# Splitting the last four down-projections of batch 0, with the up-projection's runs side by side

## The chip, the cores and the metric

The kernel runs on one core of a Trainium2 chip. Five engines work there side by side, each with its own queue in order: TensorE (PE) multiplies matrices, VectorE (DVE) and ScalarE (ACT) work elementwise, GpSimd (POOL) does so too but more slowly, and SyncE (SP) issues the transfers (DMA) from memory. The metric is the device time of one execution in microseconds (us). The kernel before takes 740.15 us, the median of three runs (739.81 to 740.30).

## The reference

An attention through a small pack, followed by a feed-forward layer with the Mish activation, all in float32:

```python
def sm_attn(qq, kk, vv):                       # softmax attention
    s = scale * np.matmul(qq, kk.transpose(0, 1, 3, 2))
    a = np.exp(s - np.max(s, axis=-1, keepdims=True))
    a = a / (np.sum(a, axis=-1, keepdims=True) + 1e-09)
    return np.matmul(a, vv)
p_packed = sm_attn(p, k, v)                    # p: 8 x 8 x 32 x 64
attn = sm_attn(q, p_packed, p_packed)          # q, k, v: 8 x 8 x 576 x 64
x = attn.transpose(0, 2, 1, 3).reshape(4608, 512)
h = x @ w_in                                   # w_in: 512 x 2048
g = h * np.tanh(np.log1p(np.exp(h)))           # Mish (h itself in the softplus above 20)
out = g @ w_out                                # w_out: 2048 x 512
```

The two weights arrive as float64 and are narrowed to float32 by the kernel.

## The kernel before

**Blocks.** The hidden width of 2048 is cut into 16 groups f of 128 columns (`NF`). One block t is the work for one group of one batch: t = 16 b + f. A block computes the up-projection of its group (`Group.up`, two runs: columns 0 to 255 and 256 to 575 of the batch's 576 tokens, into the two PSUM tiles `ps_h`), the Mish on ACT (`mish`, into `act`; the last 64 tokens go to `g_rest`), and the down-projection of an earlier group (`down(dn, c)`, four products c = 0 to 3 of 128 tokens each, accumulated in `acc` over all 16 groups). The earlier group lies one block back up to t = 16 and two blocks back from then on (`lag`).

**Two forms of a product.** Where `hi` and `lo` exist, an operand is split into a rounded part and the remainder, and three products in the type float32r (hi·hi, hi·lo, lo·hi; lines 801 to 803, and 763 for the up-projection) stand for one float32 product. Batch 0 has its down-projection in plain float32 (line 821, two instructions for each product); from batch 1 on it is split: `halves` makes `hi` and `lo` of `act` on DVE, and `split_wo(i)` makes those of group i's output weights, hi on ACT (line 114) and lo on DVE (line 115), at t = 16 + i.

**Packed weights.** The second attention has only 32 packed values for each head, so that x @ w_in is a product of its weights `aT_hi`, `aT_lo` with packed weights `wp` (packed values times w_in). `packed_half` makes them for batch 0 in every odd block (line 681 on PE, then `wp_hi` on ACT and `wp_lo` on DVE, lines 713 and 714), `packed_w` for four groups at a time for the later batches (lines 692 and 693). The PSUM pool `ps_a` has two tiles, which the packing and the attention share.

**Weights of batch 0.** The 32 pieces of w_in and w_out come in while batch 0 runs. Each passes a staging tile `w_st` of a ring of `STB` = 8 (SP, lines 641 and 675), is unpacked by `words` (ACT, lines 650 and 651; POOL, 652 and 656) and put together by `join` (DVE, lines 662 and 667). `join(n)` ends with `fetch(n + STB)`: a piece's tile is free when its `words` are done. At block t stand `join(2t + 5)` and, at the block's end, `words(2t + 9)`; pieces are counted from 0 here.

**Attention of batch 1.** It is a generator, advanced at marked places of the blocks t = 4 to 14 (three times in an even block, once in an odd one). Its loads of q, k and v stand in the same SP queue as the weights: k in t = 0 and 2, q and v in t = 4 and 5. Among its steps: the first exponentials at the end of t = 6, the second ones (`rise`, line 303) in t = 13, and in t = 14 the sum, the division, and for each of two head groups the transpose back (line 335), `upper` (ACT, line 338, `aT_hi`) and `lower` (DVE, line 341, `aT_lo`).

**Order.** PE's order is the program's throughout. Up to t = 15 that of the other engines is so too (`by_hand`); from then on a planner orders them. A block of t = 4 to 15 is written as: down 0, up run 0, advance, join, down 1, packed weights (odd blocks), down 2, advance, up run 1, halves, words, down 3, and an advance at the end of even blocks.

Of the kernel before, what the change touches and what calls it, by code (L numbers as in the profile page):

```python
# [17 lines left out]
GB = 3  # L18
KVB = 8
KQB = 5  # L20
STB = 8
WB = 4
# [7 lines left out]
HALFWAY = 8  # L30
SPLIT0 = 14
TOGETHER = 2
# [8 lines left out]
def body(  # L41
# [55 lines left out]
    PARTS = (slice(0, QC), slice(QC, S))  # L97
    wi = [[const.tile([P, 2, 2, QC], F32, name=f"wi{c}_{g}") for g in range(2)] for c in range(DF // FC)]
    stage = ExitStack()
    stg = stage.enter_context(tc.tile_pool(name="stg", bufs=STB, side="right"))  # L100
    late = []
# [6 lines left out]
    def split_wo(i):  # L108
        if i < HALFWAY:
            wo_hi[i], wo_lo[i] = [late[0].tile([P, DO], F32R, name=f"wo_{x}{i}") for x in ("hi", "lo")]  # L110
        else:
            wo_hi[i], wo_lo[i] = wo_slot(F32R, "wo_hi"), wo_slot(F32R, "wo_lo")
        both = [
            nc.scalar.copy(out=wo_hi[i], in_=wo[i]),
            nc.vector.tensor_tensor(out=wo_lo[i], in0=wo[i], in1=wo_hi[i].bitcast(F32), op=ALU.subtract),
        ]
        for x in both:
            tc.keep_in_program_order(x)

# [254 lines left out]
    class Later(Batch):  # L374
# [254 lines left out]
        def rest_rows(self):  # L629
            return out[self.b * S + MAIN:(self.b + 1) * S, :]  # L630

    class Weight:

# [5 lines left out]
        def fetch(self):  # L639
            self.st = stg.tile([P, 2 * FC], I32, name="w_st")  # L640
            nc.sync.dma_start(
                out=self.st.rearrange("p (m x) -> p m x", m=2),
                in_=w_in_v[:, 2 * self.g:2 * self.g + 2, self.n * FC:(self.n + 1) * FC],
            )
            self.dst = wi[self.n // 2][self.g][:, self.n % 2].rearrange("p m x -> p (m x)")
# [23 lines left out]
    class WeightOut(Weight):  # L669
# [3 lines left out]
        def fetch(self):  # L673
            self.st = stg.tile([P, 2 * FC], I32, name="w_st")
            nc.sync.dma_start(out=self.st, in_=w_out_v[:, self.i, :])
            self.dst = wo[self.i] = wo_slot(F32, "wo32")
# [49 lines left out]

    def split_tiles(name="g", bufs=GB):
        return [late[0].tile([P, MAIN], F32R, name=f"{name}_{n}", bufs=bufs) for n in ("hi", "lo")]

    def split(*srcs):  # L730

        hi, lo = split_tiles("r", 1)
        for n, src in enumerate(srcs):
            h, l = (x.rearrange("p (f u t) -> p u f t", u=len(srcs), f=src.shape[1])[:, n] for x in (hi, lo))
            nc.scalar.copy(out=h, in_=src)
            nc.vector.tensor_tensor(out=l, in0=src, in1=h.bitcast(F32), op=ALU.subtract)
        return hi, lo

    class Group:
# [50 lines left out]

        def halves(self):
            if self.b == 0:
                return
            self.g = split_tiles()
            hi, lo = self.g
            nc.vector.tensor_copy(out=hi, in_=self.act)  # L796
            nc.vector.tensor_tensor(out=lo, in0=self.act, in1=hi.bitcast(F32), op=ALU.subtract)  # L797
# [17 lines left out]
    def down(grp, c):  # L815
        b, f = grp.b, grp.f
        if f == 0 and c == 0:
            accs[:] = [ps_acc.tile([P, DO], F32, name=f"acc{i}", tag="acc") for i in range(NCH)]
        cs = slice(c * P, (c + 1) * P)
        if b == 0:  # L820
            nc.tensor.matmul(out=accs[c], lhsT=grp.act[:, cs], rhs=wo[f], start=f == 0, stop=f == NF - 1)  # L821
        else:
            down_one(accs[c], grp.g[0], grp.g[1], cs, f, f == 0, f == NF - 1)
        if f < NF - 1:
            return
        o = evac(accs[c], c)
        for dst, lo, hi in batches[b].rows(c):
            nc.sync.dma_start(out=dst, in_=o[lo:hi, :])
# [85 lines left out]
    with tc.manual_schedule(engines={mybir.EngineType.PE}):  # L914
# [53 lines left out]
        for t in range(n_groups + LAG):  # L968
# [28 lines left out]
            if t == NF:  # L997
                by_hand.close()
            if t == SPLIT0:
                stage.close()  # L1000
                late.append(ctx.enter_context(tc.tile_pool(name="late", bufs=1, side="right", reuse_waits="tile")))
            if 0 <= t - NF < NF:
                split_wo(t - NF)
            chunk = b == 0 and f % 2 == 1 and f < NF - 1
            if t == 0:
# [12 lines left out]
                join(3)  # L1018
            if dn:
                down(dn, 0)  # L1020
            if 2 <= t < FLOATS:
                grp.up_floats((0,), (0, 1))
                first.upper(t - 2)
            elif grp and t >= FLOATS:
                grp.up(0)
# [4 lines left out]
            if t <= 13:  # L1030
                join(2 * t + 5 + t // 12)
            if dn:
                down(dn, 1)
            if chunk:
                if t < FLOATS - 1:
                    packed_floats(f // 2 + 1, 0)
                    wps[0, f // 2 + 1] = packed_floats(f // 2 + 1, 1)
                else:
                    wps[0, f // 2 + 1] = packed_half(f // 2 + 1)
            if dn:  # L1040
                down(dn, 2)
            if t:
                advance(gen)
            if 2 <= t < FLOATS:
                grp.up_floats((1,), (0, 1))
                first.lower(t - 2)
            elif grp and t >= FLOATS:
                grp.up(1)
# [7 lines left out]
            if last:  # L1056
                flush()
                down_rest(dn)
            if dn:
                down(dn, 3)  # L1060
# [40 lines left out]
```

## Time and profile before

| | |
|---|---|
| median of three runs | 740.15 us |
| profiled execution: time | 739.97 us |
| its span, from the first instruction to the last | 738.2 us |
| granted TensorE clock over the span | 0.999 |
| DVE busy, of the span | 57% |
| ACT busy, of the span | 40% |
| POOL busy | 54.7 us, all before 111 us |
| float32 products of batch 0 (line 821) | 128 instructions, 63.7 us busy |

The page of a profile gives the busy time of each engine first. PE's busy time includes time in which a product waits in the pipeline, so its share alone does not tell whether PE is the limit; its waits and the chain of work that ended last tell that. The chain is followed back from the last instruction, at each step to what released it, or to the instruction before it on the same engine; its pieces are counted from the end of one to the end of the next. The span lies inside the execution's time; 1.77 us are outside it.

Batch 0 covers the first 130 us. The 16 DMA engines are at least 94% busy in each window of 20 us up to 100 us and at most 51% in the windows of 20 us from there to 200 us.

### The profile page before, as it was taken

How to read it: one execution, taken by the hardware profiler on the slowest of the kernel's cores; microseconds unless marked ns; L12 is line 12 of the kernel's file. 1: busy time of each engine (PE TensorE's matmuls, PEld its weight loads, DVE VectorE, ACT ScalarE, POOL GpSimd, SP SyncE). 2: the span in 40 equal slices, each digit the busy share in tenths (PEclk: the TensorE clock that was granted, in tenths of full speed). 3: DMA queues.
4: the chain of work that ended last, by engine and by line, in shares of the span. 5: the costliest groups of instructions: out<-in, count | busy, mean ns of one | idle time of the engine just before them, and what ended most of it. 6: DMA issues, size and time to landing. Idle time of an engine off the chain costs nothing.

```text
span 738.2 us, 12575 instructions
## 1 busy us (share of the span) xinstructions
PE 725.0 (98%) x5140; PEld 558.6 (76%) x5140; DVE 424.4 (57%) x727; ACT 296.5 (40%) x692; POOL 54.7 (7%) x71
## 2 busy tenths in 40 slices
PE   8899999999999999999999999999999999999997
PEld 7555555778887878887887878878788787888885
DVE  4998778848646465455734566373834638342332
ACT  4866745544433343252522425343422425232221
POOL 0585440000000000000000000000000000000000
PEclk9999999999999999999999999999999999999999
DMA  9999960735004540144202451043101100010002
GB/s 244 307 275 242 297 112 16 149 55 111 1 16 94 87 79 1 58 72 98 33 1 72 72 110 21 36 87 65 33 1 44 29 2 1 0 58 1 1 1 71
DMA packets 186601, 56.32 MB, mean 76 GB/s; under 512 B 173488, under 2 KB 175792, under 8 KB 186544
## 3 DMA queue, kind: packets, MB, share of 16 engines
q1 hardware_dynamic: 186544, 55.53, 31.9%
q8 instruction: 40, 0.66, 0.4%
q14 instruction: 17, 0.14, 0.1%
HBM read 46.07 MB, written 9.44 MB: 75 GB/s over the span
## 4 chain that ended last, share of the span: by engine, by line
PE 94%; DVE 2%; ACT 2%; DMA 1%; issue 1%; SPq 0%; ACTq 0%; DVEq 0%
PE ps_h L763 26%; PE acc L801 15%; PE acc L803 14%; PE acc L802 14%; PE acc L821 6%; PE ps_w L681 4%; PE ps_s L444 2%; PE ps_rest L803 2%; PE ps_rest L802 2%; PE ps_rest L801 2%; PE ps_h L510 1%; PE ps_h L885 1%; PE ps_h L775 1%; DMA w_st<-in_moe_w_in_dram 1%; PE ps_a L491 1%
## 5 line engine op out<-in xcount | busy, mean ns | idle before, releaser
L785 ACT ACTIVATE g<-ps_h 128x256 f32<-128x256 f32 (+2 forms) x256 | 97.5, 384 | 302.5 <-PE ps_h L763 282.4
L801 PE MATMUL acc<-wo_hi,g_hi 128*128 128x512 f32 x448 | 181.3, 405 | 0.0
L803 PE MATMUL acc<-wo_hi,g_lo 128*128 128x512 f32 x448 | 177.1, 395 | 0.0
L802 PE MATMUL acc<-wo_lo,g_hi 128*128 128x512 f32 x448 | 176.8, 395 | 0.0
L763 PE MATMUL ps_h<-aT_hi,wp_hi 128*128 128x256 f32 x496 | 157.3, 317 | 0.4 <-ACT g L785 0.4
L796 DVE CAST g_hi<-g 128x512 fp32r<-128x512 f32 x112 | 47.5, 424 | 184.7 <-ACT g L785 184.4
L763 PE MATMUL ps_h<-aT_lo,wp_hi 128*128 128x256 f32 x496 | 146.3, 295 | 0.0
L763 PE MATMUL ps_h<-aT_hi,wp_lo 128*128 128x256 f32 x496 | 146.2, 295 | 0.0
L801 PEld LDWEIGHTS acc<-wo_hi,g_hi 128*128 128x128 f32 x448 | 84.2, 188 | 40.3 <-issue 20.8
L763 PEld LDWEIGHTS ps_h<-aT_hi,wp_hi 128*128 128x128 f32 x496 | 93.4, 188 | 18.0 <-issue 6.1
L763 PEld LDWEIGHTS ps_h<-aT_lo,wp_hi 128*128 128x128 f32 x496 | 93.5, 188 | 14.5 <-issue 5.7
L803 PEld LDWEIGHTS acc<-wo_hi,g_lo 128*128 128x128 f32 x448 | 84.1, 188 | 21.5 <-DVE g_lo L797 2.0
L763 PEld LDWEIGHTS ps_h<-aT_hi,wp_lo 128*128 128x128 f32 x496 | 93.5, 188 | 0.0
L802 PEld LDWEIGHTS acc<-wo_lo,g_hi 128*128 128x128 f32 x448 | 84.1, 188 | 9.2
L797 DVE TENSOR_TENSOR g_lo<-g,g_hi 128x512 fp32r<-128x512 f32 x112 | 77.3, 690 | 5.8
L821 PE MATMUL acc<-wo,g 128*128 128x512 f32 x128 | 63.7, 605 | 1.0 <-DVE wo L667 0.6
L693 DVE TENSOR_TENSOR wp_lo<-ps_w,wp_hi 128x512 fp32r<-128x512 f32 x56 | 36.1, 684 | 17.6 <-ACT wp_hi L692 17.6
L692 ACT CAST wp_hi<-ps_w 128x512 fp32r<-128x512 f32 x56 | 30.1, 591 | 36.9 <-PE ps_w L681 36.9
L681 PE MATMUL ps_w<-wi,ppT 64*32 64x512 f32 (+1 forms) x576 | 37.9, 553 | 2.4 <-DVE wi L667 2.4
L821 PEld LDWEIGHTS acc<-wo,g 128*128 128x128 f32 x128 | 21.5, 189 | 18.8 <-issue 12.7
L787 ACT ACTIVATE g_rest<-ps_h 128x64 f32<-128x64 f32 x128 | 28.2, 220 | 0.0
L803 PE MATMUL ps_rest<-wo_hi,r_lo 128*128 128x512 f32 x64 | 25.2, 393 | 0.0
(125 smaller groups left out, 726.7 us busy)
## 6 DMA issues: line engine op xcount, KB each, us to landing
w_st<-in_moe_w_in_dram SPq DMA_DIRECT2D x16, 512.0 KB, 7.8
w_st<-in_moe_w_out_dram SPq DMA_DIRECT2D x16, 512.0 KB, 6.9
k_n<-in_k_dram SPq DMA_DIRECT2D x56, 144.0 KB, 3.2
q_n<-in_q_dram SPq DMA_DIRECT2D x56, 144.0 KB, 3.1
v_n<-in_v_dram SPq DMA_DIRECT2D x56, 128.0 KB, 2.9
out_dram<-o SPq DMA_DIRECT2D x28, 256.0 KB, 2.0
k_t<-in_k_dram SPq DMA_DIRECT2D x4, 288.0 KB, 4.6
v_t<-in_v_dram SPq DMA_DIRECT2D x4, 288.0 KB, 7.5
```

The lines of the kernel that those rows point to most:

```text
L681: nc.tensor.matmul(out=ps[h * NP:(h + 1) * NP, :], lhsT=ppTb[row:row + D, g, h * NP:(h + 1) * NP], rhs=w[row:row + D], start=True, stop=Tr ...
L692: nc.scalar.copy(out=hi, in_=ps)
L693: nc.vector.tensor_tensor(out=lo, in0=ps, in1=hi.bitcast(F32), op=ALU.subtract)
L763: nc.tensor.matmul(out=ps, lhsT=w[:, fs], rhs=a[:, g, cs], start=(n == 0), stop=(n == 5))
L785: nc.scalar.activation(out=self.act[:, a:a + m], in_=ps[:, :m], func=AF.Mish)
L787: nc.scalar.activation(out=self.g_rest[self.b % 2][self.f // 4][:, self.f % 4, :], in_=ps[:, m:n], func=AF.Mish)
L796: nc.vector.tensor_copy(out=hi, in_=self.act)
L797: nc.vector.tensor_tensor(out=lo, in0=self.act, in1=hi.bitcast(F32), op=ALU.subtract)
L801: nc.tensor.matmul(out=acc, lhsT=hi[:, cs], rhs=wh, start=start, stop=False)
L802: nc.tensor.matmul(out=acc, lhsT=hi[:, cs], rhs=wl, start=False, stop=False)
L803: nc.tensor.matmul(out=acc, lhsT=lo[:, cs], rhs=wh, start=False, stop=stop)
L821: nc.tensor.matmul(out=accs[c], lhsT=grp.act[:, cs], rhs=wo[f], start=f == 0, stop=f == NF - 1)
```

## The change

- **Down-projection.** The groups f = 12 to 15 of batch 0 (`PAIRS0` = 12) use the split form. Their output weights are split at t = 12 to 15, hi on ACT and lo on POOL, into tiles of the pool `kept`; `halves` makes hi of `act` on ACT and lo on DVE in these blocks. The splits at t = 28 to 31 go away.
- **Order.** In t = 4 to 16 both up runs stand behind down 1. In t = 13 to 16 the down-projection is in two parts: down 0 and 1 behind the join and the weights' split, down 2 and 3 at the block's end.
- **Staging.** The ring has 7 tiles in place of 8, four of them in the pool `kept` and three in `gpairs`; the first are used again for the split output weights of f = 12 to 15, the second for `hi` and `lo` of `act` in all later blocks.
- **Join.** At t = 9 one piece less is joined at the usual place, and that piece behind the packed weights.
- Split output weights of groups 0 to 3, in place of 0 to 7, have tiles of their own; the others use the tiles that float32 weights leave.

```diff
-STB = 8
+STB = 7
+KEPT = 4
...
-SPLIT0 = 14
+PAIRS0 = 12
+LATE0 = 14
...
+    kept = ctx.enter_context(tc.tile_pool(name="kept", bufs=KEPT, side="right"))
+    gpairs = ctx.enter_context(tc.tile_pool(name="gpairs", bufs=STB - KEPT, side="right"))
     stage = ExitStack()
-    stg = stage.enter_context(tc.tile_pool(name="stg", bufs=STB, side="right"))
+    stg = stage.enter_context(tc.tile_pool(name="stg", bufs=WB, side="right"))
...
     def split_wo(i):
-        if i < HALFWAY:
+        if i >= PAIRS0:
+            both = kept.tile([P, 2, DO], F32R, name="wo_pair", tag="w_st")
+            wo_hi[i], wo_lo[i] = both[:, 0], both[:, 1]
+        elif i < HALFWAY - KEPT:
             wo_hi[i], wo_lo[i] = [late[0].tile([P, DO], F32R, name=f"wo_{x}{i}") for x in ("hi", "lo")]
         else:
             wo_hi[i], wo_lo[i] = wo_slot(F32R, "wo_hi"), wo_slot(F32R, "wo_lo")
         both = [
             nc.scalar.copy(out=wo_hi[i], in_=wo[i]),
-            nc.vector.tensor_tensor(out=wo_lo[i], in0=wo[i], in1=wo_hi[i].bitcast(F32), op=ALU.subtract),
+            (nc.gpsimd if i >= PAIRS0 else nc.vector).tensor_tensor(
+                out=wo_lo[i], in0=wo[i], in1=wo_hi[i].bitcast(F32), op=ALU.subtract
+            ),
         ]
...
+    fetched = []
+
+    def staged():
+        fetched.append(1)
+        pool = kept if (len(fetched) - 1) % STB < KEPT else gpairs
+        return pool.tile([P, 2 * FC], I32, name="w_st", tag="w_st")
...
-    def split_tiles(name="g", bufs=GB):
-        return [late[0].tile([P, MAIN], F32R, name=f"{name}_{n}", bufs=bufs) for n in ("hi", "lo")]
+    def split_tiles(pool, name, tag=None):
+        both = pool.tile([P, 2, MAIN], F32R, name=name, tag=tag or name)
+        return both[:, 0], both[:, 1]
...
         def halves(self):
+            if self.b == 0 and self.f < PAIRS0:
+                return
+            self.g = split_tiles(gpairs, "g_pair", "w_st")
+            hi, lo = self.g
             if self.b == 0:
-                return
-            self.g = split_tiles()
-            hi, lo = self.g
-            nc.vector.tensor_copy(out=hi, in_=self.act)
+                nc.scalar.copy(out=hi, in_=self.act)
+            else:
+                nc.vector.tensor_copy(out=hi, in_=self.act)
             nc.vector.tensor_tensor(out=lo, in0=self.act, in1=hi.bitcast(F32), op=ALU.subtract)
...
-        if b == 0:
-            nc.tensor.matmul(out=accs[c], lhsT=grp.act[:, cs], rhs=wo[f], start=f == 0, stop=f == NF - 1)
+        if b == 0 and f < PAIRS0:
+            nc.tensor.matmul(out=accs[c], lhsT=grp.act[:, cs], rhs=wo[f], start=f == 0, stop=False)
...
-            if 0 <= t - NF < NF:
+            if 0 <= t - NF < PAIRS0:
                 split_wo(t - NF)
...
-            if dn:
+            late_down = dn and dn.b == 0 and dn.f >= PAIRS0
+            if dn and not late_down:
                 down(dn, 0)
...
-            elif grp and t >= FLOATS:
+            elif grp and t > NF:
                 grp.up(0)
             if chunk:
                 flush()
             else:
                 advance(gen)
             if t <= 13:
-                join(2 * t + 5 + t // 12)
+                join(2 * t + 5 + t // 12 - (t == 9))
+            if PAIRS0 <= t < NF:
+                split_wo(t)
+            if late_down:
+                down(dn, 0)
             if dn:
                 down(dn, 1)
+            if grp and FLOATS <= t <= NF:
+                grp.up(0)
+                grp.up(1)
             if chunk:
...
                     wps[0, f // 2 + 1] = packed_half(f // 2 + 1)
-            if dn:
+                    if t == 9:
+                        join(2 * t + 5)
+            if dn and not late_down:
                 down(dn, 2)
             if t:
                 advance(gen)
...
-            elif grp and t >= FLOATS:
+            elif grp and t > NF:
                 grp.up(1)
             if grp:
                 grp.halves()
...
+            if late_down:
+                down(dn, 2)
             if dn:
                 down(dn, 3)
```

More of the change, by code (lines that the diff above doesn't have):

```diff
@@ L114, in split_wo @@
             nc.scalar.copy(out=wo_hi[i], in_=wo[i]),
-            nc.vector.tensor_tensor(out=wo_lo[i], in0=wo[i], in1=wo_hi[i].bitcast(F32), op=ALU.subtract),
-        ]
-        for x in both:
-            tc.keep_in_program_order(x)
+            (nc.gpsimd if i >= PAIRS0 else nc.vector).tensor_tensor(
+                out=wo_lo[i], in0=wo[i], in1=wo_hi[i].bitcast(F32), op=ALU.subtract
+            ),
+        ]
+        if i < PAIRS0:
+            for x in both:
+                tc.keep_in_program_order(x)
     w_in_v = w_in.bitcast(I32).rearrange("(m p) f -> p m f", p=P)
@@ L639, in fetch @@
         def fetch(self):
-            self.st = stg.tile([P, 2 * FC], I32, name="w_st")
+            self.st = staged()
             nc.sync.dma_start(
@@ L673, in fetch @@
         def fetch(self):
-            self.st = stg.tile([P, 2 * FC], I32, name="w_st")
+            self.st = staged()
             nc.sync.dma_start(out=self.st, in_=w_out_v[:, self.i, :])
@@ L725, in body @@
     whole = {}
-    def split_tiles(name="g", bufs=GB):
-        return [late[0].tile([P, MAIN], F32R, name=f"{name}_{n}", bufs=bufs) for n in ("hi", "lo")]
+    def split_tiles(pool, name, tag=None):
+        both = pool.tile([P, 2, MAIN], F32R, name=name, tag=tag or name)
+        return both[:, 0], both[:, 1]
     def split(*srcs):
-        hi, lo = split_tiles("r", 1)
+        hi, lo = split_tiles(late[0], "r")
         for n, src in enumerate(srcs):
@@ L998, in body @@
                 by_hand.close()
-            if t == SPLIT0:
+            if t == LATE0:
                 stage.close()
                 late.append(ctx.enter_context(tc.tile_pool(name="late", bufs=1, side="right", reuse_waits="tile")))
-            if 0 <= t - NF < NF:
+            if 0 <= t - NF < PAIRS0:
                 split_wo(t - NF)
```

## The prediction

> **What bounds the kernel now.** I read the page first, then who TensorE (PE) waits for, then the chain of work that ended last between 84 and 135 us, where the changed blocks lie, and last the queues of ScalarE (ACT), VectorE (DVE) and SyncE (SP) around each place where PE could wait. The page:
>
> ```profile
> span 738.2 us, 12575 instructions
> ...
> PE 725.0 (98%) x5140; PEld 558.6 (76%) x5140; DVE 424.4 (57%) x727; ACT 296.5 (40%) x692; POOL 54.7 (7%) x71
> ...
> PE 94%; DVE 2%; ACT 2%; DMA 1%; issue 1%; SPq 0%; ACTq 0%; DVEq 0%
> ```
>
> PE is the bound almost everywhere; ahead of its queue stands next to nothing. From 40 to 140 us its waits are these, by engine, line, releaser, total, times, longest:
>
> ```profile
> PE ps_pp L526 <- DVE wp_lo L714: 1.2, 1, 1.2
> ...
> PE acc L821 <- ACT g L785: 0.4, 1, 0.4
> ```
>
> So whatever leaves PE's work is gained, and every new wait of PE is lost in full. The chain through the changed blocks (start, length, what):
>
> ```profile
> 101.90 1.72 PE acc L821 x4
> ...
> 107.76 1.72 PE acc L821 x4
> ...
> 111.05 0.59 PE ps_w L681 x16
> 111.64 1.06 PE acc L821 x2
> ...
> 119.47 1.02 PE ps_w L681 x16
> ...
> 129.87 0.86 PE acc L821 x2
> 130.73 1.59 PE ps_h L763 x12
> 132.33 0.23 PE acc L801
> 132.56 0.24 PE acc L802
> 132.79 0.23 PE acc L803
> ```
>
> One float32 down-projection product is two instructions and takes 0.86; three products of the split form take 0.70; both up-projection runs of a block take 1.59; the packing takes 0.59 (half) or 1.02 (batch 1), and the product behind it 0.20 more (1.06 against 0.86). Block t=12 starts at 101.90 + 0.86 = 102.76, t=13 at 108.62, and t=16 ends at 129.87 + 0.86 = 130.73. The chain counts a product from the end of the one before, which is some 0.2 after its operand is ready.
>
> **The change on PE.** Blocks f=12 to 15 have 4 products each: 16 × (0.86 − 0.70) = **2.5 us saved**. The up runs side by side change nothing in PE's own time: 101.90 to 130.73 shows no extra for a float32 product beside a split one (1.72 per four everywhere), and the packing has one switch before and after.
>
> The Trainium skill, "TensorE: Matmul & The Clock Gate", section "Back-to-back issue gap", has a warm gap of N/2.4 + 2.5 ns, 216 ns for 512 columns. By it, as an estimate, the split product would take 0.65, the saving would be 3.4 and my time 742.3. The rows stand at 0.23 to 0.24 each, so here the trace decides against it and it gets no chance.
>
> **The staging ring, 8 to 7.** SP works in order, and each join now fetches one piece less ahead. Counted from the first, pieces 19 and 20 are those at 58.66, 21 and 22 those at 68.53:
>
> ```profile
> 47.65 10.91 SPq L383 DMA_DIRECT2D q_n<-in_q_dram  x8
> 58.66 1.17 SPq L641 DMA_DIRECT2D w_st<-in_moe_w_in_dram  x2
> 59.87 8.57 SPq L391 DMA_DIRECT2D v_n<-in_v_dram  x10
> 68.53 1.02 SPq L675 DMA_DIRECT2D w_st<-in_moe_w_out_dram  x2
> ...
> L675 SPq DMA_DIRECT2D w_st<-in_moe_w_out_dram x4: 376/470/553, 68.5 to 71.3; - x4
> ...
> DMA to landing us min/median/max: 4.2/6.2/8.1
> ```
>
> The first of the two at 58.66 landed 4.6 after its issue, by the same view of L641 (58 to 60 us):
>
> ```profile
> DMA to landing us min/median/max: 4.6/4.9/5.2
> ```
>
> At t=4 the fetch stands between the loads of q and of v. It now ends with piece 19, so piece 20 goes behind the ten v transfers. Piece 21 was issued there and landed at 68.53 + 4.2 = 72.7; pieces 21 to 26 land (71.3 + 8.1 − 72.7)/5 = 1.34 apart, and one piece less is ahead, so piece 20 lands at about 71.4 (72.7 if SP does not move up). Piece 18 moves behind the q loads in the same way and lands near 58.66 + 4.6 − 1.3 = 62.0; ACT unpacks it at 64.0 (first row below), so it is in time. ACT before:
>
> ```profile
> 64.00 0.68 ACT L650 ACTIVATE wo<-w_st 128x512 f32<-128x512 f32 x1
> ...
> 69.87 0.69 ACT L650 ACTIVATE wi<-w_st 128x512 f32<-128x512 f32 x1
> ...
> 71.15 1.28 ACT L472 ACT_TABLE_LOAD   x1
> ...
> 74.92 0.38 ACT L785 ACTIVATE g<-ps_h 128x256 f32<-128x256 f32 x1
> ...
> 73.94 1.02 PE L821 MATMUL acc<-wo,g 128*128 128x512 f32 x2
> 75.36 1.13 PE L821 MATMUL acc<-wo,g 128*128 128x512 f32 x2 [0.39 <-ACT g L785]
> ```
>
> 69.87 is piece 20's unpacking. Behind it in ACT's queue are the exponentials of batch 1 with two table loads (71.15 to 74.92) and Mish of f=7, for which PE already waits (the last two rows, of PE: 75.36 where 73.94 + 0.86 was possible). With the piece at 71.4 the Mish starts at 71.4 + 1.15 + 3.77 = 76.35 and PE's product at 76.8: **+1.4**. The transposes behind it then wait some 0.35 for the low weights, which come later by the same cause. Against this the join moved behind the packed weights at t=9 takes two DVE instructions (0.65 each at least, more beside POOL) from in front of the subtraction that ended the 1.2 wait: **−1.2**. Together **+0.5** by t=10. Bounds: −1.8 if the piece is in time (the 1.2 gone, and the 0.6 before 75.36), +1.8 if it lands at 72.7.
>
> **The late blocks.** A product at block t+1 now needs act, then the ACT copy hi, then the DVE subtraction lo of f=t. Their costs, from the same operations elsewhere, with those of the weights' split:
>
> ```profile
> 125.27 0.62 ACT L114 CAST wo_hi<-wo 128x512 fp32r<-128x512 f32 x1
> ...
> 131.36 0.69 DVE L797 TENSOR_TENSOR g_lo<-g,g_hi 128x512 fp32r<-128x512 f32 x1
> ...
> L317 POOL TENSOR_TENSOR a<-a,sm x1: 1158/1158/1158, 22.1 to 22.1; 128x576 f32<-128x576 f32 x1
> ```
>
> POOL is idle after 111 us, so its four subtractions (near 1.1 each) are ready a block ahead and cost PE nothing, but for f=15, where it is close. The cover of the copy is c2 and c3 of the block before, 1.4 of PE. What stands in ACT's and DVE's queues ahead of it:
>
> ```profile
> 111.73 0.65 ACT L713 CAST wp_hi<-ps_w 128x256 fp32r<-128x256 f32 x2 [1.12 <-PE ps_w L681]
> 112.39 1.28 ACT L303 ACT_TABLE_LOAD   x1
> 113.69 1.16 ACT L303 ACTIVATE a<-a 128x1152 f32<-128x1152 f32 x1
> ...
> 114.89 1.35 DVE L308 TENSOR_REDUCE sm<-a 128x36 f32<-128x1152 f32 x1 [0.36 <-ACT a L303]
> 116.99 0.42 DVE L736 TENSOR_TENSOR r_lo<-g_rest,r_hi 128x256 fp32r<-128x256 f32 x1 [0.75 <-ACT r_hi L735]
> ...
> 120.21 0.72 ACT L338 CAST aT_hi<-at 128x576 fp32r<-128x576 f32 x1 [2.97 <-DVE at L335]
> ...
> 121.75 0.78 DVE L335 STREAM_TRANSPOSE at<-a 128x576 f32<-128x576 f32 x1
> ...
> 123.20 1.05 ACT L692 CAST wp_hi<-ps_w 128x512 fp32r<-128x512 f32 x2
> ```
>
> - t=12 starts 0.5 late; lo(12) follows the DVE's three joins and costs about 0.2. t=13 starts at 109.3.
> - t=13: two products 1.4, up 1.6, packing 0.6: 112.9. In the program the advance that issues batch 1's second exponential stands between the packing and the halves, so ACT does the wp_hi casts, the table load and the exponential first: 113.0 + 3.1 (111.73 to 114.85) = 116.1, then hi(13) until 116.75. PE is through c2, c3 at 112.9 + 0.2 + 1.4 = 114.5 and streams at 116.95: **2.45**. lo is ready 0.69 after hi, while the third product is due 0.47 after the first: **0.25** more.
> - t=14 runs to 116.95 + 1.65 + 1.6 + 1.4 + 1.2 = 122.85. DVE's sum L308 stands behind lo(13), so it starts at 117.5, 2.6 late. From it to aT_hi are 5.3, less 0.75 for a wait on the rest rows that I take as gone: 122.1. hi(14) is behind aT_hi: 122.1 + 0.6 + 0.63 = 123.3, streamed at 123.5: **0.7 + 0.25**. Behind lo(14) waits aT_lo on DVE, and behind that the second transpose.
> - t=15 ends at 122.85 + 0.95 + 4.4 = 128.2. lo(14) 124.0, aT_lo and transpose 1.5, second aT_hi 0.65, wp_hi 0.95, wo_hi[15] 0.63, two Mish with the rest 0.7, hi(15) 0.63: 129.05, streamed at 129.25: **1.05 + 0.25**.
> - t=16 ends at 128.2 + 1.3 + 4.4 = 133.9 against 130.73.
>
> **Sum**: −2.5 + 0.5 + 0.2 + 2.7 + 0.95 + 1.3 = **+3.15**. Behind 133 us the queues are as before and PE is never late by more than 0.6, so the shift stays. The four splits that leave t=28 to 31 were beside PE. The profiled execution took 739.97 (span 738.2 and 1.77 around it); the median of the runs is 740.15, 0.18 more. 739.97 + 3.15 = 743.1, and on the median's side 743.2.
>
> **The rivals.**
> - **The copies find cover** (the other side, faster). Place: ACT at t=13 and t=14. If hi(13) goes ahead of the exponential it is done at 113.65 + 0.63 = 114.3, in time; then hi(14) must also pass aT_hi. One alone only moves the wait to the next block. With both, the late blocks keep 0.7 of lo waits: 739.97 − 2.5 + 0.5 + 0.7 = 738.7, or 736.4 with the early piece in time. For it: ACT is busy 40% and has room. Against it: before, every ACT row from 111.73 to 124.14 stands in the program's order. Chance 0.21.
> - **The early piece is in time.** Then the early blocks give −1.8 and the late ones take +2.65: 740.8. It decides at a landing before 69.4, 2.0 earlier than I work out. Chance 0.18.
> - **More in the way**: the 0.75 on the rest rows comes again, hi and lo of one tile are waited for as one (0.45 more at each of three blocks), and POOL slows DVE. The row below bounds that: 0.65 alone, 1.10 at most beside POOL's unpacking, so 0.45 for each of two meetings. 743.2 + 0.75 + 0.45 + 0.9 = 745.3 with one of the three blocks. Chance 0.12.
>
> ```profile
> L662 DVE SCALAR_TENSOR_TENSOR wi<-wi,wsign x16: 648/688/1099, 19.2 to 102.1; 128x512 int32<-128x512 int32 x16
> ```
>
> The Trainium skill, "SBUF — State Buffer", section "Who interferes with whom", says that a DVE instruction with two inputs in SBUF and a GpSimd one that reads SBUF exclude each other for their whole length. By that, as an estimate, each such meeting costs up to POOL's own 1.1 and this rival reaches 746.6; the spread of the row agrees that they meet, not that the loss is whole.
>
> **How the numbers follow.** The forecast has 0.49: from a landing at 70.5 to one at 72.7, and 0.5 either way in the late chain, 741.8 to 745.0, at its likeliest 743.2. The range reaches down to the covered copies and up to most of the third rival: 738.0 to 745.3. A measurement of this kernel tells 0.2% (1.5 us) from no change. Faster: 0.11 with the early gain and most of the other 0.10: 0.2. Same: the second rival: 0.2. Slower: 0.6.
>
> **What would show it.** PE waits on L821's successors in t=14, 15 and 16, ended by the ACT copy and the DVE lo, with the first near 2.5; ACT rows in the order wp_hi, table load, exponential, hi. Split products of the late blocks at 0.70. A gap of ACT near 68 to 71 us ended by a weight DMA, and the wait on L526 gone. I am wrong if the late waits stay under 1 us together, if ACT's gap is missing, or if PE shows waits behind 134 us.

## The result, and the profile after

The changed kernel is slower. Its median is 745.74 us (four runs: 744.85, 745.65, 745.82, 746.85), that of the kernel before beside it 740.22 us; the ratio is 1.0075, with a 95% interval from 1.0063 to 1.0087. The prediction was 743.2, with a range up to 745.3. The profiled execution took 744.85, with a span of 742.9.

The page of the changed kernel (span, busy times, shares of the chain that ended last):

```profile
span 742.9 us, 12572 instructions
...
PE 723.6 (97%) x5156; PEld 560.8 (75%) x5156; DVE 425.8 (57%) x727; ACT 300.4 (40%) x696; POOL 60.1 (8%) x75
...
PE 86%; issue 4%; POOL 3%; DVE 3%; ACT 3%; DMA 1%; SPq 0%; POOLq 0%; DVEq 0%; ACTq 0%
```

PE is busy 1.4 us less (725.0 before) in a span that is 4.7 us longer: the split products did take work away from it, and more than that came back as waits. The next view lists whom PE waits for from 40 to 140 us (engine, line, releaser, total, times, longest):

```profile
PE acc L822 <- ACT g_pair L815: 3.3, 3, 2.2
PE acc L842 <- ACT g L803: 2.8, 1, 2.8
PE acc L824 <- DVE g_pair L818: 0.9, 1, 0.9
PE acc L842 <- DVE wo L684: 0.6, 1, 0.6
```

The 1.2 on L526 is gone. In place of it stand one wait of 2.8 at t = 8 (Mish behind a late piece of the weights) and four in the late blocks, which are these rows of PE's timeline (start, length, what, idle time ahead of it and its releaser):

```profile
78.17 1.12 PE L842 MATMUL acc<-wo,g 128*128 128x512 f32 x2 [2.85 <-ACT g L803]
111.81 0.50 PE L824 MATMUL acc<-wo_pair,g_pair 128*128 128x512 f32 x1 [0.94 <-DVE g_pair L818]
118.95 0.51 PE L822 MATMUL acc<-wo_pair,g_pair 128*128 128x512 f32 x1 [2.18 <-ACT g_pair L815]
...
125.26 0.50 PE L822 MATMUL acc<-wo_pair,g_pair 128*128 128x512 f32 x1 [0.37 <-ACT g_pair L815]
...
130.90 0.50 PE L822 MATMUL acc<-wo_pair,g_pair 128*128 128x512 f32 x1 [0.74 <-ACT g_pair L815]
```

The first is at t = 8, the others are lo(12), hi(13), hi(14) and hi(15). A wait costs some 0.25 more than the idle time shown: that time is counted from the end of the instruction before (0.40 behind its start, where the next one of a row starts after 0.23), and the second instruction behind a wait starts 0.34 after the first in place of 0.23. A late lo adds 0.15 to 0.25 where it is due just behind hi.

To see where the time went I take the length of each block, from the end of the last product of the block before to the end of its own last product in PE's timeline (t = 13 to 14, after: 116.38 + 0.40 = 116.78 is the end of t = 13).

| stretch | before | after | difference |
|---|---|---|---|
| to the start of t = 2 | 38.96 | 39.56 | +0.60 |
| t = 2 to 7 | 36.01 | 35.76 | -0.25 |
| t = 8 | 6.56 | 9.23 | +2.67 |
| t = 9 | 8.31 | 7.06 | -1.25 |
| t = 10 to 12 | 18.78 | 18.81 | 0 |
| t = 13 | 5.81 | 6.35 | +0.54 |
| t = 14 | 5.04 | 7.09 | +2.05 |
| t = 15 | 6.23 | 6.30 | +0.07 |
| t = 16 | 5.03 | 5.64 | +0.61 |
| from there to t = 25 | 43.35 | 43.34 | 0 |

The first row is start-up and not the change: in the twelve profiles of the experiments it lies between 38.41 and 40.27, whatever the kernel. The rest is +1.17 in t = 2 to 9 and +3.27 in t = 13 to 16. The median grew by 0.6 more than the profiled execution did (5.5 against 4.9); the eleventh run shows a likely cause.

### The profile page after: what moved, and what is told of

Same layout as the page of the kernel before. It is cut to its first block, busy times and chain, and to the rows that moved or that the text cites. A ratio compares the mean times of both kernels' runs of the same rounds, so it can differ in the third digit from the quotient of the medians.

```text
span 742.9 us, 12572 instructions
## 1 busy us (share of the span) xinstructions
PE 723.6 (97%) x5156; PEld 560.8 (75%) x5156; DVE 425.8 (57%) x727; ACT 300.4 (40%) x696; POOL 60.1 (8%) x75
## 4 chain that ended last, share of the span: by engine, by line
PE 86%; issue 4%; POOL 3%; DVE 3%; ACT 3%; DMA 1%; SPq 0%; POOLq 0%; DVEq 0%; ACTq 0%
PE ps_h L781 24%; PE acc L822 15%; PE acc L824 14%; PE acc L823 14%; PE ps_w L698 4%; PE ps_s L454 2%; PE ps_rest L824 2%; PE ps_rest L823 2%; PE ps_rest L822 2%; PE acc L842 2%; POOL wsign L673 1%; PE ps_h L520 1%; POOL wo L669 1%; DMA k_t<-in_k_dram 1%; PE ps_a L501 1%
## 5 line engine op out<-in xcount | busy, mean ns | idle before, releaser
L817 DVE CAST g_pair<-g 128x512 fp32r<-128x512 f32 x112 | 47.5, 424 | 185.0 <-ACT g L803 184.8
L781 PE MATMUL ps_h<-aT_hi,wp_hi 128*128 128x256 f32 x496 | 150.9, 304 | 0.0
L822 PE MATMUL acc<-wo_hi,g_pair 128*128 128x512 f32 x336 | 136.4, 406 | 0.0
L824 PE MATMUL acc<-wo_hi,g_pair 128*128 128x512 f32 x336 | 133.1, 396 | 0.3 <-DVE g_pair L818 0.3
L823 PE MATMUL acc<-wo_lo,g_pair 128*128 128x512 f32 x336 | 132.4, 394 | 0.0
L822 PEld LDWEIGHTS acc<-wo_hi,g_pair 128*128 128x128 f32 x336 | 63.1, 188 | 32.5 <-issue 18.3
L818 DVE TENSOR_TENSOR g_pair<-g,g_pair 128x512 fp32r<-128x512 f32 x116 | 79.9, 689 | 6.2 <-ACT g_pair L815 3.2
L824 PEld LDWEIGHTS acc<-wo_hi,g_pair 128*128 128x128 f32 x336 | 63.1, 188 | 17.2 <-DVE g_pair L818 2.8
L823 PEld LDWEIGHTS acc<-wo_lo,g_pair 128*128 128x128 f32 x336 | 63.1, 188 | 6.7
L822 PE MATMUL acc<-wo_pair,g_pair 128*128 128x512 f32 x128 | 51.9, 405 | 3.3 <-ACT g_pair L815 3.3
L824 PE MATMUL acc<-wo_pair,g_pair 128*128 128x512 f32 x128 | 50.9, 398 | 0.9 <-DVE g_pair L818 0.9
L842 PE MATMUL acc<-wo,g 128*128 128x512 f32 x96 | 47.3, 608 | 3.4 <-ACT g L803 2.8
L823 PE MATMUL acc<-wo_pair,g_pair 128*128 128x512 f32 x128 | 50.3, 393 | 0.0
```

The source lines that it names most:

```text
L781: nc.tensor.matmul(out=ps, lhsT=w[:, fs], rhs=a[:, g, cs], start=(n == 0), stop=(n == 5))
L822: nc.tensor.matmul(out=acc, lhsT=hi[:, cs], rhs=wh, start=start, stop=False)
L823: nc.tensor.matmul(out=acc, lhsT=hi[:, cs], rhs=wl, start=False, stop=False)
L824: nc.tensor.matmul(out=acc, lhsT=lo[:, cs], rhs=wh, start=False, stop=stop)
```

## The experiments

Times are medians; the kernel before had 740.22 to 740.35 on the same chips.

| run | median us | ratio to before, 95% interval |
|---|---|---|
| e1 order alone, ring of 8 | 738.66 | 0.9981 (0.9972 to 0.9990) |
| e2 order alone, ring of 7 | 742.37 | 1.0029 (1.0017 to 1.0040) |
| e3 after, one piece fetched early | 741.26 | 1.0011 (1.0002 to 1.0021) |
| e4 after, no second exponential | 744.85 | 1.0060 (1.0045 to 1.0075) |
| e5 = e3 with early hi and lo | 739.00 | 0.9982 (0.9973 to 0.9992) |
| e6 = e5, no second exponential | 738.98 | 0.9980 (0.9971 to 0.9989) |
| e7 = e3, weights' lo on DVE | 740.79 | one run |
| e8 = e5, join and one split moved | 739.77 | 0.9995 (0.9986 to 1.0005) |
| e9 = e8, chain behind the up runs | 741.36 | 1.0017 (1.0006 to 1.0028) |
| e10 = e8, no sum and division | 738.25 | 0.9967 (0.9957 to 0.9977) |
| e11 after, once more | 749.08 | one run |
| e12 = e9, lo(14) on POOL | 740.87 | 1.0005 (0.9996 to 1.0015) |

### Order alone, and the ring

The first two take the kernel before and give it only the new order (both up runs behind down 1, the moved join), with the ring as it was and with a ring of 7:

```diff
-            elif grp and t >= FLOATS:
+            elif grp and t > NF:
                 grp.up(0)
...
-                join(2 * t + 5 + t // 12)
+                join(2 * t + 5 + t // 12 - (t == 9))
             if dn:
                 down(dn, 1)
+            if grp and FLOATS <= t <= NF:
+                grp.up(0)
+                grp.up(1)
...
                     wps[0, f // 2 + 1] = packed_half(f // 2 + 1)
+                    if t == 9:
+                        join(2 * t + 5)
...
-STB = 8          # second kernel only
+STB = 7
```

> The kernel before with the order alone: both up runs behind down 1 in t=4 to 16, and the one join of t=9 behind the packed weights; ring of 8, no late split. My theory: the two early waits go (1.2 at t=9, 0.6 at t=8), about 738.4 us. Rival (the order itself costs PE, because the packing comes later in a block): 740 to 741.5.

> As the order alone, with a ring of 7. My theory: piece 20 goes behind the v loads and lands near 72.7, ACT waits about 3 us for it at t=6, and the time is 2.5 to 3.0 us above the order with a ring of 8, about 741.3 us. Rival (the ring costs nothing, the early loss of the changed kernel comes from elsewhere): within 0.5 us of the ring of 8. It also tells whether the 0.6 us that the changed kernel is late at t=4 already belongs to the ring: then the block t=4 starts 0.6 later here too.

The order alone gains 1.7 and beats the kernel before; its profile shows PE waiting for nothing from 60 to 110 us. Block t = 8 takes 5.92 there (6.56 before) and t = 9 takes 7.06 (8.31). The ring alone then costs 3.7. In the second kernel, PE's waits, ACT's row of the late piece, and PE's stretches of 4 us around it (length, busy PE and PEld, DVE, ACT, POOL, granted clock, DMA share, GB/s):

```profile
PE acc L821 <- ACT g L785: 3.9, 1, 3.9
```

```profile
73.38 0.67 ACT L650 ACTIVATE wi<-w_st 128x512 f32<-128x512 f32 x1 [4.28 <-DMA w_st<-in_moe_w_in_dram]
```

```profile
74.00:78.00 4.00, 0.97 (x3) 0.14 (x1) 0.00 (x0) 3.95 (x5) 1.23 (x2) 0.97 1.05 403
78.00:82.00 4.00, 3.17 (x7) 1.87 (x8) 2.53 (x4) 3.99 (x11) 1.48 (x3) 0.50 0.72 264
82.00:86.00 4.00, 4.00 (x16) 2.83 (x15) 4.00 (x5) 1.16 (x4) 1.62 (x2) 0.68 0.75 256
```

The piece lands at 73.4, PE waits 3.9 for the Mish behind it, and then it works at half clock for several microseconds. That second part was in nobody's sum. This profiled execution is the slowest of seven (745.46; the others took 741.35 to 743.55), so the median of 742.37 holds less of it.

### One piece fetched ahead

The changed kernel, with piece 20 fetched at t = 4 ahead of the loads of v, where the ring of 8 had it:

```diff
                 join(2 * t + 5 + t // 12 - (t == 9))
+                if t == 4:
+                    fetch(21)
```

> The changed kernel with piece 20 fetched in t=4 ahead of the v loads (its tile is free by then); ring of 7 kept. My theory: piece 20 lands before 66 us, the 3.2 us of ACT waiting for it go, and with them about 3 us: 742.7 us. Rival (the v transfers, now behind one more piece, make the attention late): 744.5 or more, with a new wait at the values of t=9 or t=10.

It gives back 4.5, more than the 3.0 expected, and the early wait is gone (t = 8 takes 5.90). What is left of PE's waits of the change is the late ones, as they were:

```profile
PE acc L822 <- ACT g_pair L815: 3.3, 3, 2.2
...
PE acc L824 <- DVE g_pair L818: 1.3, 2, 0.9
```

With that the result splits into three parts: order -1.7 (e1 against before), split products with their waits, and what else the ring of 7 costs, +2.6 (e3 against e1), late piece +4.5 (after against e3); together +5.4 of the 5.5 measured.

### The exponential ahead of hi(13)

The changed kernel, with `rise` left out for batch 1:

```diff
         def rise(self, gs):
+            if self.b == 1:
+                return
```

> The changed kernel without batch 1's second exponential (left out; its softmax is then not one). My theory: hi of f=13 was queued behind it and its two table loads, so PE's wait at t=14 (2.45) goes, and the chain of DVE behind it comes 2.4 earlier, so the waits at t=15 and t=16 stay near 0.5 and 1.0: about 2.7 us less, 743.0 us. Rival (the copy and the subtraction themselves are what PE waits for): under 0.5 us less, 745.3.

It came out at 744.85, 0.9 less than the changed kernel where 2.7 was expected. The wait for hi(13) on ACT is gone, and another stands in its place. PE's row of t = 14:

```profile
119.52 0.50 PE L826 MATMUL acc<-wo_pair,g_pair 128*128 128x512 f32 x1 [1.88 <-DVE g_pair L820]
```

It waits for lo(13), which stands on DVE behind the two joins of t = 13 and wp_lo, and which takes 1.35 there in place of 0.69. POOL's subtraction of group 14's weights, which now comes earlier too, lies across it; DVE's row and then POOL's:

```profile
118.11 1.35 DVE L820 TENSOR_TENSOR g_pair<-g,g_pair 128x512 fp32r<-128x512 f32 x1
```

```profile
117.66 1.26 POOL L122 TENSOR_TENSOR wo_pair<-wo,wo_pair 128x512 fp32r<-128x512 f32 x1 [3.76 <-ACT wo_pair L121]
```

So behind the queue of ACT stood a queue of DVE, and 0.66 of the 1.88 is the meeting with POOL. The blocks t = 13 to 16 are 0.54 shorter than in the changed kernel (24.84 against 25.38); the rest of the 0.9 is within the scatter of the two kernels' runs (744.01 to 745.42 and 744.85 to 746.85). My reason in the prediction (hi behind the exponential) was right for the wait that I saw, and wrong as the price of the exponential.

### hi and lo ahead of the other work

From here on the early fetch stays in. In t = 12 to 15 `halves` goes right behind the up runs, ahead of wp_hi, wp_lo and the exponential:

```diff
                 grp.up(0)
                 grp.up(1)
+                if PAIRS0 <= t < NF:
+                    grp.halves()
...
             if grp:
-                grp.halves()
+                if not PAIRS0 <= t < NF:
+                    grp.halves()
```

> The version with the early fetch, and in t = 12 to 15 hi and lo are issued right behind the up runs, ahead of the packing's copies and the exponential. Theory now: the waits at t = 13 and 14 are order, but behind them stands batch 1's attention chain (exponential, sum, division, transposes, aT_hi, aT_lo, wp_hi, wp_lo) which these edits do not start earlier. Then lo(12) costs some 0.2 (1.2 to 0.9 before), hi(13) is in time, lo(13) waits 1.2 behind the join on DVE, and hi(15), which stays behind aT_hi and wp_hi, takes a wait of about 2.5: in all 1.2 less than 741.3, about 740.0. Rival, only the order counts: hi(13), lo(12), hi(14) and hi(15) all in time, 4 less, about 737. Rival, order does not count (hi starts no earlier): 741.3.

> The same with batch 1's second exponential left out (its table loads too). If the exponential on ACT is what sets the end of the chain, about 2.5 less than the same kernel with it. If DVE's queue sets it (the sum waits behind the join of t = 13, lo(13) and wp_lo until about 114 in any case), about 0.9 less, and the sum starts within 0.3 of where it starts with the exponential.

> The version with the early fetch, with the four subtractions of the output weights on DVE in place of POOL. If POOL is what makes DVE's joins at t = 12 long, the last of them takes 0.65 in place of 1.76 and the wait for lo(12) (0.93) goes to 0.2 although DVE has 0.65 more to do; the time is about 741.2, since the other subtractions then stand in DVE's queue ahead of the sum at t = 14. If the join is long for another reason, it stays at 1.7 and the wait grows to 1.6.

The fifth kernel is 2.3 below the third, 1.0 better than I expected. PE's waits in its timeline:

```profile
107.22 0.50 PE L824 MATMUL acc<-wo_pair,g_pair 128*128 128x512 f32 x1 [0.20 <-DVE g_pair L818]
113.88 0.50 PE L824 MATMUL acc<-wo_pair,g_pair 128*128 128x512 f32 x1 [1.24 <-DVE g_pair L818]
124.83 0.50 PE L822 MATMUL acc<-wo_pair,g_pair 128*128 128x512 f32 x1 [1.05 <-ACT g_pair L815]
```

lo(12) 0.2 and lo(13) 1.2 are as expected, hi(14) is in time, and hi(15) waits 1.05 (2.5 expected). So order did account for most of the late waits. Yet this kernel, with three waits left, is level with the order alone (739.00 and 738.66): the 2.5 that the split saves are more than used up by them (t = 13 to 16 take 23.17, where e1 takes 22.10), and what e1 loses later evens it out.

Without the exponential nothing more is gained (738.98), where 0.9 less was expected even if DVE's queue decides; the blocks t = 13 to 16 are 0.18 shorter (22.99 against 23.17). DVE's sum (L318 with the exponential, L320 without, since the edit adds two lines) tells why; first the fifth kernel, then the sixth:

```profile
114.41 1.34 DVE L318 TENSOR_REDUCE sm<-a 128x36 f32<-128x1152 f32 x1
```

```profile
114.20 1.33 DVE L320 TENSOR_REDUCE sm<-a 128x36 f32<-128x1152 f32 x1
```

The sum starts at the same place, 0.2 apart as the two profiles are throughout: DVE reaches it only then, behind the join, lo(13) and wp_lo. At this place DVE's queue, not ACT's exponential, sets when the attention goes on.

The seventh kernel is the third (late hi and lo) with the weights' subtraction back on DVE. The last unpacking row of t = 12 on DVE, in the changed kernel and then in the seventh, with POOL's row of the former between them:

```profile
108.66 1.76 DVE L684 CUSTOM_DVE_ANT_0 wo<-wo,wround 128x1024 uint16<-128x1024 uint16 x1
```

```profile
108.17 1.71 POOL L122 TENSOR_TENSOR wo_pair<-wo,wo_pair 128x512 fp32r<-128x512 f32 x1
```

```profile
104.66 0.68 DVE L684 CUSTOM_DVE_ANT_0 wo<-wo,wround 128x1024 uint16<-128x1024 uint16 x1
105.26 0.68 DVE L122 TENSOR_TENSOR wo_pair<-wo,wo_pair 128x512 fp32r<-128x512 f32 x1
...
106.63 0.96 DVE L818 TENSOR_TENSOR g_pair<-g,g_pair 128x512 fp32r<-128x512 f32 x1
```

The join's instruction takes 0.68 in place of 1.76, so the subtraction on POOL is what stretched it. But DVE has 0.68 more to do, and lo(12) itself now meets POOL's unpacking (0.96); the wait went from 0.93 in the third kernel to 0.77 only, not to 0.2. Its one run, 740.79, also holds a stretch of half clock behind the wait for hi(13) (t = 14 takes 8.37, where the third kernel takes 7.09), so its time says little about the subtraction.

### Taking the next waits away

The eighth kernel moves one of the two joins of t = 13 behind the packing and group 15's split of the weights from t = 15 to t = 14. The ninth also moves the end of batch 1's attention and its packing behind the up runs of t = 15. The tenth is the eighth without the sum and the division; the twelfth is the ninth with lo(14) on POOL.

```diff
-                join(2 * t + 5 + t // 12 - (t == 9))
+                join(2 * t + 5 + t // 12 - (t in (9, 13)))
...
-                    if t == 9:
-                        join(2 * t + 5)
+                    if t in (9, 13):
+                        join(2 * t + 5 + t // 12)
...
-            if PAIRS0 <= t < NF:
+            if PAIRS0 <= t < LATE0 + 1:
                 split_wo(t)
...
+                if t == LATE0:
+                    split_wo(t + 1)
```

The ninth adds:

```diff
-            if chunk:
+            if chunk or t == NF - 1:
                 flush()
...
-            if t:
+            if t == NF - 1:
+                finish(gen)
+                wps[1, 0] = packed_w(1, 0)
+            elif t:
                 advance(gen)
...
-            if grp and f % 4 == 2 and (b or f == NF - 2):
+            if t == NF - 2:
+                advance(gen)
+            elif grp and f % 4 == 2 and b:
```

The tenth and the twelfth:

```diff
         def share(self, gs):
+            if self.b == 1:
+                return
...
-            nc.vector.tensor_tensor(out=lo, in0=self.act, in1=hi.bitcast(F32), op=ALU.subtract)
+            by = nc.gpsimd if self.b == 0 and self.f == LATE0 else nc.vector
+            by.tensor_tensor(out=lo, in0=self.act, in1=hi.bitcast(F32), op=ALU.subtract)
```

> The version with early hi and lo, and at t = 13 one of its two joins behind the packing (lo(13) is then ready 1.25 earlier on DVE), and the weights' split of group 15 moved from t = 15 to t = 14. The wait for lo(13) (1.24) goes to 0.2 or less and hi(15) is 0.5 earlier. Theory, batch 1's attention chain sets hi(15), since ACT and DVE work on it in order: PE comes 1.3 earlier to hi(15) and waits for it about 1.8 where it waited 1.05; the time falls by the 0.5 alone, to about 738.5. Rival, each wait is its own and goes by itself: 1.7 less, 737.3.

> The same, and the last part of batch 1's attention (second aT_hi and aT_lo) with its packing (PE, wp_hi, wp_lo) moved from the end of t = 14 to t = 15, behind its up runs, Mish, hi and lo. Theory: hi(15) and lo(15) then come before PE needs them, wp_lo ends some 0.4 later than before the move and PE reaches the up runs of t = 16 just then: the waits behind t = 13 go but for 0.5 or less, about 737.0. Rival, the chain's end only moves the wait: PE waits for wp_lo at t = 16 for what it gained, 738.5 again. Rival, the attention's tiles hold PE's packing up: above 739.

> The version with one join and the split of group 15 moved, with the sum, reciprocal and division of batch 1's second attention left out (3.3 us of DVE). Theory, the late blocks wait for DVE's and ACT's work on that attention: lo(14) no longer stands behind it, its wait (2.04) goes to 0.3 or less, aT_hi and wp_hi come 3 earlier and hi(15) is in time: 2.5 to 4 less than the 739.8 with it, 736 to 737.3. Rival, the weights' subtraction on POOL (1.95 beside DVE) or the order of ACT's casts holds lo(14): 1 or more of the wait stays, 739.

> The version with the chain behind the up runs of t = 15, and lo(14) subtracted on POOL, which is idle there, in place of DVE. Theory: the wait for lo(14) goes from 2.36 to about 0.8, the clock stays at 1.00, hi(15) and lo(15) are in time, and block 16 starts some 3.5 earlier: 737.6 to 738.5, level with the order alone (738.66). Rival, POOL beside DVE's division is so slow that the wait stays above 2 and the clock falls again: 740 or more.

The wait for lo(13) goes to 0.3 or less in all four, and in the eighth, ninth and twelfth the time does not fall. PE comes earlier to t = 15 and waits there for lo(14). The eighth kernel's row of PE, and its stretches (length, busy PE, clock, DMA share, GB/s):

```profile
121.67 0.76 PE L824 MATMUL acc<-wo_pair,g_pair 128*128 128x512 f32 x1 [2.04 <-DVE g_pair L818]
```

```profile
119.00:121.00 2.00, 0.63 (x2) 1.00 0.00 0
121.00:123.00 2.00, 1.33 (x3) 0.69 0.01 4
123.00:125.00 2.00, 2.00 (x9) 0.50 0.00 0
125.00:127.00 2.00, 2.00 (x12) 0.96 0.00 0
```

DVE does the sum, the division and the transpose ahead of lo(14) (at 120.68), so the gain of 1.2 turns into a wait of 2.0, and that one puts the clock at half. The theory had the wrong place (hi(15)), and 739.77 is above both its number and the rival's. The half clock is not all of it: three of the ten runs have a mean clock of 1.000 and take 739.32 to 739.72, no less than the fifth kernel's 739.00. The ninth kernel waits 2.36 at the same place, also with the clock at half behind it. PE then waits for neither hi(15) nor lo(15) (t = 16 takes 4.35, where the fifth kernel takes 5.95), as the theory had it, but PE also comes later, so that what the chain's move is worth in time stays open. Without sum and division (e10) that wait is 0.3 or less and the time 1.5 lower; the next one appears at once:

```profile
124.78 0.50 PE L824 MATMUL acc<-wo_pair,g_pair 128*128 128x512 f32 x1 [1.27 <-ACT g_pair L817]
```

It is hi(15), behind aT_hi and wp_hi. So even with 3.3 us of DVE work taken out the gain is 1.5, where 2.5 or more were expected. On POOL (e12) the subtraction lo(14) runs beside DVE's division and takes twice what such a subtraction takes there otherwise; POOL's rows:

```profile
115.07 1.29 POOL L122 TENSOR_TENSOR wo_pair<-wo,wo_pair 128x512 fp32r<-128x512 f32 x1 [5.10 <-ACT wo_pair L121]
118.00 2.47 POOL L819 TENSOR_TENSOR g_pair<-g,g_pair 128x512 fp32r<-128x512 f32 x1 [1.63 <-ACT g_pair L815]
```

and DVE's division:

```profile
117.98 1.36 DVE L327 TENSOR_TENSOR a<-a,sm 128x1152 f32<-128x1152 f32 x1
```

PE waits 1.82 for it, the clock falls to half again, and the rival's 740 or more is what came, at a wait somewhat shorter than its 2. The two of its ten runs with a mean clock of 1.000 take 739.51 and 739.44, still above the 738.5 of the theory.

### The changed kernel once more

> The changed kernel as it is, once more, for the granted clock behind its longest waits (2.8 at t = 8 and 2.2 at t = 13 in the first profile, both with the clock at 1.00). Theory: where such a wait exceeds about 2, the clock may fall to half for some 3.5 us, and the scatter of this kernel's times (744.85 to 746.85) is that. Then a run at clock 0.998 shows a window of 0.5 to 0.7 behind one of the two waits and a run at 1.000 shows none. Rival: the scatter is the start-up or the landing of the pieces, with the clock at 1.00 everywhere.

It took 749.08, 4.2 more than in its first profile. PE's rows at t = 8 and t = 14:

```profile
79.83 2.07 PE L842 MATMUL acc<-wo,g 128*128 128x512 f32 x2 [3.81 <-ACT g L803]
...
123.05 0.80 PE L822 MATMUL acc<-wo_pair,g_pair 128*128 128x512 f32 x1 [2.18 <-ACT g_pair L815]
```

(The expectation names the second wait by t = 13; it stands at the start of t = 14.) In the first profile the clock stood at 1.00 behind both, and the second wait was as long to the hundredth (2.18). The same wait can thus leave the clock alone or halve it.

The traces show what decides. In all fourteen profiled executions the clock changes only at whole multiples of 3.41 us, counted from its first change to full speed; that first change lies anywhere from 4.15 to 6.81 (here at 6.81; 78.49 is 21 multiples later, 122.86 is 34). Cut into pieces at these multiples, this execution shows (length, busy PE, clock, DMA share, GB/s):

```profile
75.08:78.49 3.41, 0.94 (x3) 1.00 1.03 395
78.49:81.90 3.41, 2.07 (x3) 0.50 1.01 396
81.90:85.31 3.41, 3.41 (x12) 0.50 0.75 241
...
119.45:122.86 3.41, 1.42 (x6) 1.00 0.01 2
122.86:126.27 3.41, 3.22 (x9) 0.50 0.03 5
```

and the first profile, whose clock first changed at 5.32:

```profile
73.59:77.00 3.41, 1.73 (x4) 1.00 1.04 399
77.00:80.41 3.41, 2.24 (x9) 1.00 1.02 397
...
114.55:117.96 3.41, 2.22 (x23) 1.00 0.01 2
117.96:121.37 3.41, 2.42 (x12) 1.00 0.02 5
```

From the first change to 700 us, each piece at full clock in which PE was idle for 1.99 to 2.80 (eight of them, in e2, e4, e7, e8, e9, e12 and twice here) has half clock behind it, and none with 1.68 or less has; what lies between was not met. A piece at half clock with 1.06 or 1.34 of idle time is followed by another one, a piece with 0.32 or less by full clock. So a wait of some 2 us halves the clock when it falls into one piece, and not when a boundary cuts it: the first profile's 2.18 is cut at 117.96 into 1.19 and 0.99, and this one's lies in one piece but for 0.19.

At t = 8 the block takes 12.63, 3.40 more than in the first profile; 0.96 of that is longer waiting, so the half clock costs 2.4. At t = 14 it costs next to nothing: t = 13 to 16 take 25.49 against 25.38, since PE, being later, waits less for hi(14) and hi(15). So the theory of the clock holds for this run, and the rival's landing has a part in it, the 0.96.

## Why the prediction was wrong

The direction was right, and so was the mechanism of the late blocks (hi and lo queued on ACT and DVE). The time is 0.4 above the range because three terms were too small or left at nothing: the landing of piece 20, the clock, and lo(12).

- **Split products at 0.70.** Right: three instructions 0.23 apart, and PE's busy time falls.
- **The 1.2 wait on L526.** Right: t = 9 is 1.25 shorter, in every kernel with the new order.
- **The early piece in time: -1.8.** Right as a bound: e1 takes 12.99 for t = 8 and 9, where the kernel before took 14.87.
- **"So piece 20 lands at about 71.4": failed.** It was issued earlier, as argued, but landed at 72.7, the time that I had for the case in which SP does not move up. The view of the fetches (L658, 58 to 72 us) has 4.8 from issue to landing at least, where I took 4.2 from a neighbour that had more pieces ahead of it:

```profile
DMA to landing us min/median/max: 4.8/6.3/7.9
```

  ACT's row shows the gap that I named:

```profile
72.69 0.70 ACT L667 ACTIVATE wi<-w_st 128x512 f32<-128x512 f32 x1 [3.18 <-DMA w_st<-in_moe_w_in_dram]
```

  t = 8 and 9 cost +1.42 in the profiled execution, where the sum had +0.5 and the bound +1.8. (Block t = 8 starts 0.35 later here than before, so against the blocks the piece is 1.0 late and not 1.3.) Counted to the start of t = 8, ACT began with the piece 2.6 ahead here (75.32), and 1.6 ahead in e11 (76.02) and in e2 (74.97): the landing moves by 1 from execution to execution, and I priced one value of it.
- **Nothing for the clock: failed.** The granted clock was 0.999 before and I left it there. Behind a wait of some 2 us or more it may fall to half, and at t = 8 that costs 2.4 in e11. The other three timed runs of the changed kernel had spans of 743.7, 743.9 and 744.9 at mean clocks of 0.998, 0.998 and 0.995, the profiled one 742.9 at 1.000. Half clock in some of them would account for the late piece costing 4.5 by the medians and 3.3 by one profile (t = 8: 9.23 against 5.90 with the early fetch); no trace of these three runs shows it. The Trainium skill, "TensorE: Matmul & The Clock Gate", section "Part 1: The HAM clock gate", has the clock halved after an idle window of about 3.4 us that runs freely, without regard to the program. The traces agree with the free window: the clock changes only at multiples of 3.41 us, and one wait of 2.18 has either outcome. The window need not be idle as a whole here: 1.99 of its 3.41 was enough.
- **"lo(12) ... costs about 0.2": failed.** It cost 1.2 (0.94 and the start-up; t = 13 is 0.54 longer where 0.64 was saved). I had POOL's subtractions as free for PE, "ready a block ahead". They were in time, if not by a block (0.6 ahead of their use for f = 12, 0.24 for f = 15), but the first stretches DVE's join ahead of lo(12) from 0.68 to 1.76. The last rival had 0.45 for each meeting; here one meeting cost DVE 1.08.
- **hi(13): 2.45 and 0.25 more.** Right: t = 14 is 2.05 longer, and with the 0.64 saved that is 2.69. The order on ACT is the one written down (wp_hi, table load, exponential, hi):

```profile
115.27 0.65 ACT L730 CAST wp_hi<-ps_w 128x256 fp32r<-128x256 f32 x2
115.94 1.28 ACT L313 ACT_TABLE_LOAD   x1
117.23 1.16 ACT L313 ACTIVATE a<-a 128x1152 f32<-128x1152 f32 x1
118.30 0.60 ACT L815 CAST g_pair<-g 128x512 fp32r<-128x512 f32 x1
```

- **hi(14) 0.95, hi(15) 1.3.** Measured 0.07 + 0.64 = 0.71 and 0.61 + 0.64 = 1.25. Right. The chain from the sum to aT_hi and wp_hi held as worked out.
- **"Behind 133 us ... the shift stays".** Right for before and after. e1, with the new order alone, loses 0.6 at t = 19 (7.33, where before and after have 6.72 and 6.71), so that the split costs 2.6 by the medians and not the 3.3 that its blocks show. Behind t = 25 each kernel with the split is some 0.4 shorter than before, a little in many blocks.
- **The rival "the copies find cover".** It did not happen by itself, and where it was made to happen (e5) it was worth 2.3, not the 4.5 between 743.2 and 738.7: lo(13) and hi(15) came next.
- **The working.** 740.15 + 3.15 is 743.3, where 743.2 is written, and the sums given as 76.35 and 122.85 come to 76.32 and 122.80. None of this bears on the outcome.

Late blocks, predicted +2.65, measured +3.27; early ones, predicted +0.5, measured +1.17; the start-up was 0.6 longer in this profile by chance.

What the runs show of the late blocks as a whole: hi and lo of f = 12 to 15 need ACT and DVE in the very blocks in which these do batch 1's attention in order. In the kernel before, the products needed neither. Each wait that was taken away let PE arrive earlier at the next place that needs the same two queues. No version with the split that computes the whole result came out ahead of the order alone (738.66); e10 is 0.4 below it, with the sum and the division left out, and the two intervals overlap. That none could is not shown: other lags between a block and its down-projection, or splitting two groups only, were not tried.

## What to carry to other kernels

An operand that must now be prepared by another engine costs what stands in that engine's queue ahead of it; ask the same of the second engine in line before pricing the removal of the first. Price a prefetch by the spread of its landing, not by one landing, and count half clock behind a PE wait of 2 us or more as a case of its own, which one profile may miss. When a change bundles an order, a buffer and an arithmetic change, time them apart: here the order alone was worth 0.2%, and the other two hid it.

## What was not expected of the hardware

- The granted clock falls to 0.50 behind pauses of PE of 1.8 to 3.9 us, not always (2.85 and 2.18 at 1.00 in one execution, 3.81 and 2.18 at 0.50 in another). It does so on a grid of 3.41 us that starts anew in each execution, when PE was idle for 1.99 or more of one piece of it (1.68 did not do it), and stays for 3.41 us (six times) or 6.83 (e2, and t = 8 in e11). At t = 8 that costs 2.4 for 6.83 us (e11) and 1.5 for 3.41 (e4: a block of 10.02 with a wait of 2.16, against 9.23 with 2.85); where PE waits for other engines anyway, nearly nothing.
- DVE and POOL shut each other out, where the prediction took the spread of 0.65 to 1.10 as a bound. In e12 the subtraction on POOL starts 0.02 behind DVE's division (117.98, 1.36 long), and its 2.47 are that division's time and its own 1.29 one after the other, less 0.18; the division is not slowed, and DVE's transpose behind it, with one input, takes its usual 0.78 beside POOL. In the changed kernel DVE's unpacking takes 1.76 (0.68 alone) and ends 0.54 behind POOL's subtraction. The Trainium skill, "SBUF — State Buffer", section "Who interferes with whom", has two such instructions exclude each other for their whole length. I gave that to the last rival as a page's estimate and held that the loss is not whole; these rows agree with the page.
